# Holding the second group's loads behind most of the output weights, which come in four pieces

## The chip, the core and the metric

The kernel runs on one core of one Trainium2 chip. The metric is the device time of one execution in microseconds; the runs of a kernel are compared by their median. The kernel before was run six times: median 223.87 us, from 222.33 to 224.88 us.

## What is computed

A gated linear attention is followed by a small MLP. There are 4 batches, 8 heads, 768 positions and a head size of 48. Cut to what matters, the reference is:

```python
f = 1.0 / (1.0 + np.exp(-f_logit))
for t in range(S):
    state = f[:, :, t, :, None] * state + np.einsum('bhd,bhe->bhde', k[:, :, t], v[:, :, t])
    y[:, :, t] = np.einsum('bhd,bhde->bhe', q[:, :, t], state)
x = y.transpose(0, 2, 1, 3).reshape(B * S, H * D)      # 3072 x 384
h = x @ w_in                                           # w_in: 384 x 2048
out = (h * sigmoid(h)) @ w_out                         # w_out: 2048 x 384
```

All inputs lie in the chip's memory (HBM) in float32. q, k, v and f_logit have 4.7 MB each, the two weight matrices 3.1 MB each.

## The kernel before, in words

**Groups.** The 768 positions are cut into six groups of 128 (the index g). A group holds all four batches (b from 0 to 3), 512 rows of the MLP. For each group and batch, `logs` and `decays` make the decay factors from f (ACT and TensorE), `scale_k`, `scale_q` and `values` make bf16 copies of k, q and v (POOL, DVE, POOL), `transposes`, `scores`, `outputs` and `state` do the attention, and `turn` lays its result out for the MLP. `mlp_in` multiplies by w_in and applies the SiLU; `mlp_out` multiplies by w_out, copies a row block out of PSUM on ACT and stores it by a DMA that ACT issues.

**Loads of q, k, v and f.** `load` (L84) issues one DMA on SP. In groups 0 and 1 each input comes in two halves, batches 0 and 1 (`FIRST`) and batches 2 and 3 (`SECOND`), 393 KB each; from group 2 on each comes whole, 786 KB. SP issues nothing else, so its order is the order of all these loads: the eight halves of group 0, then by `load_all` (after the `turn` loop) the eight of group 1 in the order f, k, q, v FIRST, f, k, q, v SECOND, then group 2, and so on. One head's row of 48 float32 values is 192 bytes, and that is what a packet of this queue carries. The queue is called q1 in the profile. The tiles `f_ld`, `k_ld`, `q_ld`, `v_ld` have two buffers each, so group 1 can be loaded while group 0 is in use.

**Loads of the weights.** `load_w_in` and `load_w_out` are generators whose DMAs POOL issues; they turn float32 into bf16 on the way. w_in comes in four pieces of 512 columns, w_out in two pieces of eight row blocks each (n from 0 to 7 and from 8 to 15). This queue is q0 in the profile. Its packets carry 1024 bytes (w_in) or 768 bytes (w_out) as written. The first w_in piece is issued after `scale_k(0, 2)`, the rest after `scale_k(0, 3)`.

**Order.** The program is written out in its final order for each engine (`manual_schedule`), and each engine takes its own instructions in that order. Around the change it is: attention of group 0; `mlp_in(0)` for the first two batches, then for the other two; on ACT the table load `exp_ln_tables` and `logs(1, FIRST)`; `mlp_out(0)`, whose row block of one batch needs all sixteen n of w_out in order, two row blocks by itself and then in turns with `prep(1, FIRST)` (`decays`, `scale`, `lasts`), `logs(1, SECOND)`, `attend(1, FIRST)` and the decays of the second half. `interleave_gen` takes from several streams by the share of their cost that is spent.

Of the kernel before, what the change touches and what calls it, by code (L numbers as in the profile page):

```python
# [11 lines left out]
BF16 = mybir.dt.bfloat16  # L12
# [18 lines left out]
def chain(*gens):  # L31
    for gen in gens:
        yield from gen
# [8 lines left out]
def kernel(  # L42
# [10 lines left out]
    nc = tc.nc  # L53
# [7 lines left out]
    NT = d_ff // 128  # L61
    MT = B * C

    singles = ctx.enter_context(tc.tile_pool(name="singles", bufs=1))
# [14 lines left out]
    def load(g, name, b0=0, b1=B):  # L79
        if (g, name) not in loaded:  # L80
            loaded[g, name] = ld.tile([C, B, H, D], F32, name=f"{name}_ld", tag=f"{name}_ld")
        t = loaded[g, name]
        src = SRC[name].rearrange("b h s d -> s (b h) d")[g * C:(g + 1) * C, b0 * H:b1 * H]
        nc.sync.dma_start(out=t[:, b0:b1].rearrange("p b h d -> p (b h) d"), in_=src)  # L84
# [16 lines left out]
    w_out_sb = singles.tile([128, NT, d_model], BF16)  # L101
    triu = singles.tile([C, C], BF16)
    ident = singles.tile([C, C], BF16)
    ones = singles.tile([C, 1], BF16)
    zeros = singles.tile([C, NP * 2 * D], BF16)

    def load_w_in():
        src = moe_w_in.rearrange("(ko ki) n -> ki ko n", ki=128)
        for n in range(0, d_ff, 512):
            nc.gpsimd.dma_start(out=w_in_sb[:, :, n:n + 512], in_=src[:, :, n:n + 512])  # L110
            yield

    def load_w_out():
        src = moe_w_out.rearrange("(ko ki) n -> ki ko n", ki=128)
        for n in range(0, NT, 8):
            nc.gpsimd.dma_start(out=w_out_sb[:, n:n + 8, :], in_=src[:, n:n + 8, :])
            yield

    def exp_ln_tables():
        nc.scalar.preload_act_table_set("natural_log_exp_and_others")  # L120
# [5 lines left out]
    def logs(g, lo, hi):  # L126

        f = loaded[g, "f"][:, lo:hi]
        nc.scalar.activation(f, f, AF.Exp, scale=-1.0)  # L129
        nc.scalar.activation(lf[g % 3][:, lo:hi, :, 0:D], f, AF.Ln, bias=1.0)  # L130

    def decays(g, b):

        cs = cps.tile([C, H, D], F32, name="cs", tag="cs")
        nc.tensor.matmul(cs, triu, lf[g % 3][:, b, :, 0:D], start=True, stop=True)  # L135
        ias[b] = wk.tile([C, H, D], F32, name="ia", bufs=4)
        nc.scalar.activation(ias[b], cs, AF.Exp, scale=1.0)  # L137
        aas[b] = wk.tile([C, H, D], F32, name="a", bufs=4)
        nc.scalar.activation(aas[b], cs, AF.Exp, scale=-1.0)  # L139

    def scale_k(g, b):
        nc.gpsimd.tensor_mul(ki[g % 2][:, b, :, 0:D], loaded[g, "k"][:, b], ias[b])  # L142

    def scale_q(g, b):
        nc.vector.tensor_mul(qg[g % 2][:, b, :, 0:D], loaded[g, "q"][:, b], aas[b])  # L145
# [6 lines left out]
    def values(g, b, engine=None):  # L152
        src, dst = loaded[g, "v"][:, b], vb[g % 2][:, b]
        if engine is nc.scalar:
            nc.scalar.copy(dst, src)
        else:
            nc.gpsimd.tensor_copy(dst, src)  # L157
# [39 lines left out]
    def evac(engine, dst, src):  # L197
        if engine is nc.scalar:
            nc.scalar.copy(dst, src)
        else:  # L200
            nc.vector.tensor_copy(dst, src)  # L201
# [19 lines left out]
    def turn(g, b, engine=None):  # L221

        x_ps = yps.tile([128, KT, C], BF16, name="x_ps", tag="yd")
        for t in range(KT):
            nc.tensor.transpose(x_ps[:, t, :], ysb[b][:, 128 * t:128 * (t + 1)], ident)  # L225
        if g not in xT:
            xT[g] = gk.tile([128, KT, B, C], BF16, name="xT")
        evac(engine, xT[g][:, :, b, :], x_ps)
# [73 lines left out]
    def mlp_cost(lo, hi):  # L302
        return (hi - lo) * 4 * 650.0
# [11 lines left out]
    def prep_cost(lo, hi):  # L315
        return (hi - lo) * 1000.0 + 100.0
# [5 lines left out]
    def warm(n):  # L322

        w_ps = hps.tile([128, MT], F32, name="w_ps", tag="h_ps")
        for _ in range(n):
            nc.tensor.matmul(w_ps[:, 0:NP * 2 * D], zeros[:, 0:128], zeros, start=True, stop=True)
# [19 lines left out]
    def run(*streams):  # L346
        for _ in interleave_gen(*streams):
            pass

    def load_all(g, names="fkqv", *spans):  # L350
        for span in spans or (ALL,):
            for name in names:
                load(g, name, *span)

    with tc.manual_schedule():
        exp_ln_tables()
        nc.vector.memset(zeros, 0.0)
        nc.vector.memset(ones, 1.0)
        make_upper_triangular(nc, triu, 1.0, diag=True)
        make_identity(nc, ident)  # L360
        for t in (lf[0], qg[0], ki[0], lf[1], qg[1], ki[1], lf[2]):
            nc.vector.memset(t[:, :, :, D:64], 0.0)
        for b in range(B):
            nc.gpsimd.memset(st[b], 0.0)
        w_in, w_out = load_w_in(), load_w_out()


        warm(12)
        logs(0, *FIRST)
        for b in range(*FIRST):  # L370
            decays(0, b)
            warm(2)
            scale_k(0, b)
            scale_q(0, b)
        for b in range(*FIRST):
            values(0, b)
        logs(0, *SECOND)
        for b in range(*FIRST):
            transposes(0, b)
            warm(2)  # L380
        for b in range(*FIRST):
            scores(0, b)
            warm(3)
        decays(0, 2)
        scale_k(0, 2)
        next(w_in)
        outputs(0, 0, nc.scalar)
        decays(0, 3)
        scale_k(0, 3)
        outputs(0, 1, nc.scalar)  # L390
        for _ in chain(w_in, w_out):
            pass
        lasts(0, *ALL)
        scale_q(0, 2)
        scale_q(0, 3)
        for b in range(*FIRST):
            turn(0, b, nc.scalar)
        load_all(1, "fkqv", FIRST, SECOND)
        load_all(2)
        transposes(0, 2)  # L400
        warm(2)
        transposes(0, 3)
        for b in range(*SECOND):
            values(0, b, nc.scalar)


        in0 = mlp_in(0, *FIRST)
        scores(0, 2)
        run((part(in0, 650.0), 650.0))
        scores(0, 3)  # L410
        run((part(in0, 650.0), 650.0))
        outputs(0, 2)
        run((part(in0, 650.0), 650.0))
        outputs(0, 3)
        turn(0, 2)
        run((part(in0, 650.0), 650.0))
        turn(0, 3)
        run((in0, 2600.0))
        run((mlp_in(0, *SECOND), mlp_cost(*SECOND)), (states(0, *ALL), B * D_COST))


        exp_ln_tables()
        logs(1, *FIRST)
        out0 = mlp_out(0, *ALL)
        run((part(out0, 4550.0), 4550.0))
        run((part(out0, 2600.0), 2600.0), (prep(1, *FIRST), prep_cost(*FIRST)))
        logs(1, *SECOND)
        run((out0, 3250.0), (attend(1, *FIRST), attend_cost(1, *FIRST)),
            (chain(wait(1500.0), prep(1, *SECOND, False)), 1500.0 + prep_cost(*SECOND)))
        scales(1, *SECOND)  # L430
        load_all(3)
        att = attend(1, *SECOND)
        half = attend_cost(1, *SECOND) / 2
        run((mlp_in(1, *FIRST), mlp_cost(*FIRST)), (chain(wait(600.0), part(att, half)), half + 600.0))
        exp_ln_tables()
        logs(2, *ALL)
        run((mlp_out(1, *FIRST), mlp_cost(*FIRST)), (att, half),
            (chain(wait(1300.0), prep(2, *ALL, False)), 1300.0 + prep_cost(*ALL)))
        scales(2, *ALL)


        for g in range(1, NCH):
            span = SECOND if g == 1 else ALL
            first = [(mlp_in(g, *span), mlp_cost(*span))]
            if g + 1 < NCH:
                att = attend(g + 1, *ALL)
                total = attend_cost(g + 1, *ALL)
                half = total * 0.54
                first.append((part(att, half), half))
            run(*first)  # L450
            second = [(mlp_out(g, *span), mlp_cost(*span))]
            if g + 1 < NCH:
                second.append((att, total - half))
            if g + 2 < NCH:
                exp_ln_tables()
                logs(g + 2, *ALL)
                lead = 4000.0 if g == 1 else 2000.0
                second.append((chain(wait(lead), prep(g + 2, *ALL, g > 1)), lead + prep_cost(*ALL)))
            run(*second)
            if g == 1:  # L460
                scales(g + 2, *ALL)
            if 2 <= g + 3 < NCH:
                load_all(g + 3)
# [30 lines left out]
```

## Time and profile before

| | |
|---|---|
| median of the six runs | 223.87 us |
| the profiled execution's own time | 222.38 us |
| its span, first to last instruction | 220.6 us |
| mean granted TensorE clock in it | 0.969 |
| TensorE busy with matmuls | 188.4 us, 85% of the span |
| ACT, DVE, POOL busy | 126.2, 104.5, 46.4 us |
| moved by DMA | 27.00 MB; q1 18.88, q10 (stores) 4.72, q0 (weights) 3.15 |

The profile is of one execution. "The span in 40 slices" shows the busy share of each engine and of the 16 DMA engines over time. The timeline gives for each run of equal instructions the start, the time from the start of the first to the end of the last, the engine, the line of the kernel, the operation, output and inputs, the count, and in brackets how long the engine had been idle before and what ended that. Of the DMA engines it gives, for a stretch of time, each queue's packets, bytes and the time that its packets took, as a share of sixteen engines over the stretch; packets of one engine overlap, so the shares can sum to more than 100%. The granted clock is the share of full speed at which TensorE was let run.

### The profile page before, as it was taken

How to read it: one execution, taken by the hardware profiler on the slowest of the kernel's cores; microseconds unless marked ns; L12 is line 12 of the kernel's file. 1: busy time of each engine (PE TensorE's matmuls, PEld its weight loads, DVE VectorE, ACT ScalarE, POOL GpSimd, SP SyncE). 2: the span in 40 equal slices, each digit the busy share in tenths (PEclk: the TensorE clock that was granted, in tenths of full speed). 3: DMA queues.
4: the chain of work that ended last, by engine and by line, in shares of the span. 5: the costliest groups of instructions: out<-in, count | busy, mean ns of one | idle time of the engine just before them, and what ended most of it. 6: DMA issues, size and time to landing. Idle time of an engine off the chain costs nothing.

```text
span 220.6 us, 4190 instructions
## 1 busy us (share of the span) xinstructions
PE 188.4 (85%) x1740; PEld 117.1 (53%) x1740; DVE 104.5 (47%) x189; ACT 126.2 (57%) x209; POOL 46.4 (21%) x64
## 2 busy tenths in 40 slices
PE   6486399787778587999799998999998999999993
PEld 2244178554466355865455655555665456643461
DVE  3358352204846438886764666556673446300000
ACT  3438147836174856596667855768647671158421
POOL 4317400006220074007400066000363000000000
PEclk9679769999999999999999999999999999999999
DMA  7999999999999999999999411000011000110011
GB/s 134 187 186 190 194 189 184 197 197 230 214 186 207 176 188 226 183 196 208 210 163 197 63 73 70 5 1 3 36 71 39 0 3 36 39 71 0 0 71 71
DMA packets 105970, 27.00 MB, mean 122 GB/s; under 512 B 99296, under 2 KB 105952, under 8 KB 105952
## 3 DMA queue, kind: packets, MB, share of 16 engines
q1 hardware_dynamic: 98816, 18.88, 58.2%
q0 software_dynamic: 3680, 3.15, 8.7%
q10 hardware_dynamic: 3456, 4.72, 6.3%
q8 instruction: 13, 0.21, 0.4%
q14 instruction: 5, 0.04, 0.1%
HBM read 25.17 MB, written 4.72 MB: 135 GB/s over the span
## 4 chain that ended last, share of the span: by engine, by line
PE 61%; DMA 12%; DVE 11%; ACT 8%; POOL 3%; issue 3%; ACTq 1%; SPq 1%; DVEq 0%
PE o_ps L292 23%; PE h_ps L282 21%; DMA w_out_sb<-in_moe_w_out_dram 9%; DVE qg L145 5%; PE t_ps L178 5%; PE a_ps L188 4%; DMA q_ld<-in_q_dram 3%; DVE qk L180 2%; DVE atm L192 2%; PE y_ps L210 1%; POOL w_in_sb L110 1%; PE y_ps L214 1%; ACT o_sb L297 1%; PE cs L135 1%; PE x_ps L225 1%
## 5 line engine op out<-in xcount | busy, mean ns | idle before, releaser
L282 PE MATMUL h_ps<-xT,w_in_sb 128*128 128x256 bf16 (+1 forms) x384 | 74.8, 332 | 6.2 <-DMA w_in_sb<-in_moe_w_in_dram 3.6
L285 ACT ACTIVATE hT<-h_ps 128x512 bf16<-128x512 f32 x96 | 56.8, 597 | 32.9 <-PE h_ps L282 31.1
L292 PE MATMUL o_ps<-w_out_sb,hT 128*128 128x384 bf16 x384 | 71.9, 326 | 1.7 <-DMA w_out_sb<-in_moe_w_out_dram 1.7
L282 PEld LDWEIGHTS <-w_in_sb 128*128 128x128 bf16 x384 | 35.2, 99 | 28.5 <-issue 6.2
L142 POOL TENSOR_TENSOR ki<-k_ld,ia 128x384 bf16<-128x384 f32 x24 | 24.9, 1038 | 119.3 <-ACT ia L137 93.7
L292 PEld LDWEIGHTS <-hT 128*128 128x128 bf16 x384 | 34.9, 97 | 26.3 <-issue 6.7
L192 DVE TENSOR_TENSOR atm<-a_ps,triu 128x512 bf16<-128x512 f32 x48 | 30.9, 686 | 19.8 <-PE a_ps L188 19.8
L145 DVE TENSOR_TENSOR qg<-q_ld,a 128x384 bf16<-128x384 f32 x24 | 22.8, 977 | 22.4 <-ACT a L139 16.2
L297 ACT COPY o_sb<-o_ps 128x384 f32<-128x384 f32 x24 | 11.5, 478 | 26.7 <-PE o_ps L292 26.7
L180 DVE COPY qk<-t_ps 128x1024 bf16<-128x1024 bf16 x24 | 16.6, 690 | 18.4 <-PE t_ps L178 18.4
L137 ACT ACTIVATE ia<-cs 128x384 f32<-128x384 f32 x24 | 11.8, 491 | 20.9 <-PE cs L135 17.2
L240 DVE TENSOR_TENSOR st<-d_ps,al 48x192 bf16<-48x192 f32 x40 | 14.1, 353 | 15.9 <-PE d_ps L236 15.6
L157 POOL CAST vb<-v_ld 128x384 bf16<-128x384 f32 x22 | 15.3, 697 | 1.2 <-DMA v_ld<-in_v_dram 1.2
L135 PE MATMUL cs<-lf,triu 128*128 128x384 bf16 x24 | 7.9, 331 | 8.1 <-ACT lf L130 4.5
L178 PE MATMUL t_ps<-ident,qg 128*128 128x128 bf16 x96 | 9.7, 226 | 5.4 <-DVE qk L180 3.6
L201 DVE CAST y<-y_ps 128x384 bf16<-128x384 f32 x22 | 12.2, 553 | 4.5 <-PE y_ps L214 4.3
L178 PEld LDWEIGHTS <-qg 128*128 128x128 bf16 x96 | 7.5, 100 | 10.8 <-issue 5.4
L129 ACT ACTIVATE f_ld<-f_ld 128x768 f32<-128x768 f32 (+1 forms) x8 | 9.3, 1162 | 6.9 <-DMA f_ld<-in_f_logit_dram 6.8
L188 PE MATMUL a_ps<-qk 48*128 48x128 bf16 x192 | 10.0, 226 | 2.9 <-DVE atm L192 2.9
L139 ACT ACTIVATE a<-cs 128x384 f32<-128x384 f32 x24 | 11.6, 484 | 0.0
L214 PE MATMUL y_ps<-vb,atm 128*128 128x48 bf16 x192 | 11.6, 186 | 0.0
L188 PEld LDWEIGHTS <-qk 48*128 48x128 bf16 x192 | 5.7, 97 | 11.1 <-issue 7.0
(40 smaller groups left out, 143.3 us busy)
## 6 DMA issues: line engine op xcount, KB each, us to landing
out_dram<-o_sb ACTq DMA_DIRECT2D x24, 192.0 KB, 1.9
f_ld<-in_f_logit_dram SPq DMA_DIRECT2D x4, 768.0 KB, 11.0
k_ld<-in_k_dram SPq DMA_DIRECT2D x4, 768.0 KB, 11.4
q_ld<-in_q_dram SPq DMA_DIRECT2D x4, 768.0 KB, 11.0
v_ld<-in_v_dram SPq DMA_DIRECT2D x4, 768.0 KB, 10.8
f_ld<-in_f_logit_dram SPq DMA_DIRECT2D x4, 384.0 KB, 6.7
k_ld<-in_k_dram SPq DMA_DIRECT2D x4, 384.0 KB, 7.6
q_ld<-in_q_dram SPq DMA_DIRECT2D x4, 384.0 KB, 6.6
```

The lines of the kernel that those rows point to most:

```text
L142: nc.gpsimd.tensor_mul(ki[g % 2][:, b, :, 0:D], loaded[g, "k"][:, b], ias[b])
L145: nc.vector.tensor_mul(qg[g % 2][:, b, :, 0:D], loaded[g, "q"][:, b], aas[b])
L157: nc.gpsimd.tensor_copy(dst, src)
L178: nc.tensor.transpose(t_ps[:, j, p, :], src[i][:, b, 2 * p:2 * p + 2, :], ident)
L180: nc.vector.tensor_copy(sb, t_ps)
L188: nc.tensor.matmul(a_ps[:, r, p, :], qkT[b][lo:lo + D, 1, p, :], qkT[b][lo:lo + D, 0, p, :], start=True, stop=True)
L192: nc.vector.tensor_mul(sb[:, r], a_ps[:, r], triu[:, None, :].to_broadcast([C, NP, C]))
L214: nc.tensor.matmul(y_ps[:, 2 * p + r, :], atm[b][:, r, p, :], vb[i][:, b, 2 * p + r, :], start=not opened, stop=True, skip_group_check=True)
L240: nc.vector.tensor_mul(st[b][lo:lo + D, :, r * D:(r + 1) * D], d_ps[lo:lo + D, :, r * D:(r + 1) * D], alast[g][lo:lo + D, b, :, None].to_b ...
L282: nc.tensor.matmul(h_ps[:, j], w_in_sb[:, kk, (n + j) * 128:(n + j + 1) * 128], xT[g][:, kk, lo:hi].rearrange("p b c -> p (b c)"), start=( ...
L285: nc.scalar.activation(hT[g][:, n:n + per, lo * C:hi * C], h_ps, AF.Silu)
L292: nc.tensor.matmul(o_ps, hT[g][:, n, b * C:(b + 1) * C], w_out_sb[:, n, :], start=(n == 0), stop=(n == NT - 1))
```

## The change

w_out comes in four pieces of four row blocks in place of two of eight. A one-row tile `behind` of 64 bf16 values is added. After group 0's `turn` loop, and ahead of `load_all(1, ...)`, SP issues a DMA of 128 bytes from w_out's row block 10 into that tile. Row block 10 is in the third piece (n from 8 to 11), so this DMA waits until that piece has landed, and with it every later load on SP's queue waits. Nothing reads `behind`.

```diff
@@ -102,6 +102,7 @@
     ones = singles.tile([C, 1], BF16)
+    behind = singles.tile([1, 64], BF16)
     zeros = singles.tile([C, NP * 2 * D], BF16)
@@ -112,8 +113,8 @@
     def load_w_out():
         src = moe_w_out.rearrange("(ko ki) n -> ki ko n", ki=128)
-        for n in range(0, NT, 8):
-            nc.gpsimd.dma_start(out=w_out_sb[:, n:n + 8, :], in_=src[:, n:n + 8, :])
+        for n in range(0, NT, 4):
+            nc.gpsimd.dma_start(out=w_out_sb[:, n:n + 4, :], in_=src[:, n:n + 4, :])
             yield
@@ -395,6 +396,9 @@
         for b in range(*FIRST):
             turn(0, b, nc.scalar)
+
+
+        nc.sync.dma_start(out=behind, in_=w_out_sb[0:1, 10, 0:64])
         load_all(1, "fkqv", FIRST, SECOND)
         load_all(2)
```

## The prediction

> **What bounds the kernel now.** I read the 40 slices first: TensorE is at 9 tenths from about 60 us to the end, the DMA engines from the start to about 121 us. A change in the loads can show only where TensorE waits for one. The waits between 20 and 60 us name two such places: the first w_in piece (3.6 us, ending at 26.19) and the second half of w_out. The timeline of PE shows the second:
>
> ```profile
> 40.73 0.81 PE L282 MATMUL h_ps<-xT,w_in_sb 128*128 128x256 bf16 x6
> 41.40 1.46 PE L292 MATMUL o_ps<-w_out_sb,hT 128*128 128x384 bf16 x8
> 44.52 4.06 PE L292 MATMUL o_ps<-w_out_sb,hT 128*128 128x384 bf16 x24 [1.65 <-DMA w_out_sb<-in_moe_w_out_dram]
> 48.41 0.33 PE L135 MATMUL cs<-lf,triu 128*128 128x384 bf16 x1
> ```
>
> The first eight matmuls use row blocks 0 to 7, then PE stands until the second half has landed. Matmuls of this run follow each other every 0.162 us (24 from 44.52 to 48.41), so eight need 1.3 us, and the start-to-start loss is 44.52 - 41.40 - 1.3 = 1.8 us. ACT in the same stretch:
>
> ```profile
> 42.20 1.28 ACT L120 ACT_TABLE_LOAD   x1
> 43.49 0.84 ACT L129 ACTIVATE f_ld<-f_ld 128x768 f32<-128x768 f32 x1
> 44.37 0.84 ACT L130 ACTIVATE lf<-f_ld 128x768 bf16<-128x768 f32 x1
> 46.01 0.48 ACT L297 COPY o_sb<-o_ps 128x384 f32<-128x384 f32 x1 [0.80 <-PE o_ps L292]
> ...
> 48.61 0.48 ACT L297 COPY o_sb<-o_ps 128x384 f32<-128x384 f32 x1 [2.12 <-PE o_ps L292]
> ...
> 49.56 0.49 ACT L137 ACTIVATE ia<-cs 128x384 f32<-128x384 f32 x1 [0.47 <-PE o_ps L292]
> ```
>
> Here ACT waits for PE, not for loads: f FIRST of group 1 landed at 21.7 (issued 14.90, 6.8 to landing) and is first used at 43.49. That slack of 22 us is what the change spends. POOL says when the weights are issued and when k and v of group 1 are used:
>
> ```profile
> 18.57 0.93 POOL L110 DMA_DIRECT2D w_in_sb<-in_moe_w_in_dram  x1
> ...
> 22.80 1.78 POOL L116 DMA_DIRECT2D w_out_sb<-in_moe_w_out_dram  x2
> 50.14 0.99 POOL L142 TENSOR_TENSOR ki<-k_ld,ia 128x384 bf16<-128x384 f32 x1 [25.55 <-DMA out_dram<-o_sb]
> 51.09 0.82 POOL L157 CAST vb<-v_ld 128x384 bf16<-128x384 f32 x1
> ```
>
> **What the queues cost each other.** The DMA view of three stretches: 12 to 18 us (q1 alone), 26 to 31 (w_in beside q1), 34 to 42 (w_out beside q1).
>
> ```profile
> q1 hardware_dynamic: 5872, 1.12, 144.6%
> ```
> ```profile
> q0 software_dynamic: 806, 0.79, 93.2%
> q1 hardware_dynamic: 810, 0.16, 27.8%
> ```
> ```profile
> q0 software_dynamic: 1535, 1.17, 92.8%
> q1 hardware_dynamic: 1536, 0.29, 33.5%
> ```
>
> Both queues send equal numbers of packets: they take turns, and as q0's are four to five times larger, w_out already has most of the time. Per engine (a sixteenth of the packets): q1 alone one packet every 6 us / 367 = 16.4 ns; a w_in packet with its q1 partner 5 / 50.4 = 99 ns; a w_out packet with its partner 8 / 95.9 = 83 ns.
>
> With q1 held, q0 runs alone, which this trace never shows. **Bounds for a w_out packet alone:** 83 ns if q1 only filled gaps; 83 - 16.4 = 67 if the partner took what it takes alone; 54 if q0's packets overlapped as q1's do alone (92.8% of 8 us over 95.9 packets is 77 ns each, by 1.45). For w_in: 99, 83, 64. I take the middle ones; the nearest row, q1 alone, prices the partner that goes.
>
> **When the third piece lands (T).** w_in is 1536 packets, 96 per engine, w_out 2048, 128 per engine. q0's first packets move at 21.9 (POOL's issue at 18.57 plus 3.3), and it loses 0.9 us near 24.5 between the first two pieces; I keep both. Middle: 96 x 83 ns = 8.0, 128 x 67 = 8.6, plus 0.9: last packet at 39.4, the third piece's 32 x 67 = 2.1 earlier, 37.3. From last packet (about 43.3) to PE's start (44.52) it took 1.2, so **T = 38.5**. Slow end: the halves landed at 39.0 (22.80 + 16.2) and 44.5, so three quarters stand at 41.8. Fast end: 96 x 64 + 128 x 54 = 13.1, plus 0.9, less 1.7, plus 1.2: 35.4.
>
> **The parts.** 1. *Four pieces for two*: two more issues of 0.9 us on POOL, until 26.4. POOL's next work is at 50.14, so nothing; without that cover 1.8 us. Row blocks 8 to 11 no longer wait for 12 to 15.
>
> 2. *w_out earlier*: in the middle case T is 38.5 and the fourth piece lands at 40.6, before PE needs them (42.7 and 43.3). The 1.8 us stall goes. At the slow end the fourth still lands at 44.5 and about 1.2 of it stays.
>
> 3. *w_in earlier*: the first piece saves 24 x 16 ns = 0.4 us, but TensorE's granted clock from 24.5 to 31.4 is 0.5, so starting 0.4 sooner saves 0.2 of full-speed work. Together **2.0**.
>
> 4. *The hold*: behind SP's waiting DMA stand all later loads; stores go by ACT's queue and are free. f FIRST lands at T + 0.4 (issue of the small DMA, from the first f_ld issue) + 4.0 (shortest f_ld issue to landing) = 42.9. With everything 2 us earlier on PE, ACT is free for the logs at about 43.3: no wait. After them come 0.84 + 0.84, the copies and store issues of two row blocks, and `ia`; `ia` follows PE's second row block and has 0.85 us of room. So f costs nothing up to T = 39.75, eats the gain one for one after that, and at T = 41.75 nothing is left. k, q, v FIRST follow at 2.1 us each (393 KB at 187 GB/s): 45.0, 47.1, 49.2, wanted at 48.1, 48.5 and 49.1, so v is even. The second four land at 51.3, 53.4, 55.5, 57.6. f SECOND is wanted at 50.4, but what needs it, `ia` of batch 2, is at 56.6; k at 57.1 and v at 58.1 are in time. Group 2 took 18 us after v SECOND (53.5 to 71.5) and is then complete at 75.6; its v is wanted at 76.6. Later groups have more room. Sum of the hold: 0 in the middle case. At the slow end f FIRST lands at 46.2 and `ia` is at 49.6, as before; v FIRST lands at 52.5, 1.4 after POOL wanted it (51.09), and `ki` of batch 1 waits behind it; from nothing to 1.0 of that reaches PE, as TensorE has the transposes of batch 0 and four MLP matmuls in between.
>
> Sum: -2.0 us; bounds -2.4 (fast end: w_in's first piece 24 x 35 ns = 0.8 sooner, worth 0.4) and +1.0 (slow end). The profiled execution has 222.38, giving 220.4; the median is 1.49 above that execution, and the same 2.0 from it gives **221.9**.
>
> **Two rules of the skill.** The page DMA: Bandwidth & Descriptors, Rules for kernel authors, says to issue a DMA early and wait for it late; by it the hold, which gives up f's 22 us of cover, should cost time. The row of f's landing at 21.7 agrees that the cover is there; by my sum it isn't all needed. Its section Bandwidth fits a POOL-issued DMA as 2.0 us plus bytes at 436 GB/s; by that w_in and three quarters of w_out (2.75 MB) would, as an estimate, take 8.3 us and T would be about 27 to 30, and the hold free by a wide margin. The 34 to 42 row, 1.17 MB in 8 us beside q1, doesn't look like it.
>
> **Rivals.**
> *The hold eats it.* q0 is paced by its own packets (93% of the time with packets of its own speaks for that) and hardly quickens: T between 40.6 and 41.8. The stall goes, and `ia` is late by as much. A milder form: in the median execution PE reaches `mlp_out` 1.5 us later than in the profiled one and the stall is only 0.3. Either gives about -0.4: 223.5.
> *Slower: f is late.* Place: ACT, waiting in `logs(1, FIRST)` with the two PSUM copies behind it, and PE behind `ia`. From T = 41.75 each us costs one. If the small DMA is released only by all of w_out at an unchanged pace, T = 44.5 and the price is 2.75: 226.6; halfway 225.3. For: q1's starts are then all at once late, v FIRST past 52. Against: PE's start at 41.40 shows that waits go by pieces, and q1's 28 to 34% share must come free somewhere.
> *q0 much faster alone* (54 ns): PE gains only 0.4 more, since the stall can't go twice: 221.5. Counted with the forecast.
>
> **Numbers.** Forecast 0.60, hold eats it 0.20, slower 0.20. About 0.5% (1.1 us) is what a measurement of this kernel tells from no change; the forecast lies beyond it, the first rival inside, the second beyond on the other side. Range: down to the fast end less the 0.6 us by which such medians may differ, 220.9; up into the slower rival to 225.4. If the forecast's mechanism holds, 221.3 to 222.6.
>
> **What the changed profile would show.** Right: PE's 32 matmuls from 41.2 in one piece; q0's packets alone from 22 to about 39.5, w_out every 67 ns per engine; no wait of ACT at `f_ld` near 43.3; `cs` of group 1 near 46.5. Wrong: SP's f_ld issue after 42; an ACT idle entry "DMA f_ld"; POOL waiting for v_ld near 50 or 77. A clock step at another time would move all of this alike and prove nothing.

## The result, and the profile after

The changed kernel has a median of 220.66 us (28 runs, 218.60 to 223.34); the kernel before, beside it and over all its runs, 224.19 us (63 runs). The ratio is 0.988, 95% interval 0.986 to 0.991: about 2.6 us faster (2.0 to 3.2), where 2.0 was forecast. The ratio compares the executions of each kernel that lie within 1.5% of its quickest, which is why it says less than the 3.5 us between the two medians. The profiled execution took 220.56 us with a span of 218.8, 1.8 less than before.

PE's timeline of the changed kernel, to be laid beside the four lines of before:

```profile
24.23 0.83 PE L283 MATMUL h_ps<-xT,w_in_sb 128*128 128x256 bf16 x6 [1.88 <-DMA w_in_sb<-in_moe_w_in_dram]
...
27.96 1.46 PE L283 MATMUL h_ps<-xT,w_in_sb 128*128 128x256 bf16 x6 [1.22 <-DMA w_in_sb<-in_moe_w_in_dram]
...
41.00 5.36 PE L293 MATMUL o_ps<-w_out_sb,hT 128*128 128x384 bf16 x32
46.20 0.33 PE L136 MATMUL cs<-lf,triu 128*128 128x384 bf16 x1
```

The wait for w_out is gone: 32 matmuls in one piece, and `cs` of group 1 at 46.20 instead of 48.41. `mlp_out` itself begins only 0.4 us earlier. The last 64 matmuls of the kernel, before and after:

```profile
206.71 10.56 PE L292 MATMUL o_ps<-w_out_sb,hT 128*128 128x384 bf16 x64
```
```profile
204.48 10.56 PE L293 MATMUL o_ps<-w_out_sb,hT 128*128 128x384 bf16 x64
```

So the 2.2 us gained at `cs` reach the last matmuls unchanged. The span is only 1.8 us shorter, as it ended 3.2 us after the last store was issued and not 2.8.

SP's timeline shows the hold, and ACT's what it costs:

```profile
37.57 0.58 SPq L401 DMA_DIRECT2D behind<-w_out_sb  x1
38.19 0.57 SPq L84 DMA_DIRECT2D f_ld<-in_f_logit_dram  x1
```
```profile
43.09 0.84 ACT L130 ACTIVATE f_ld<-f_ld 128x768 f32<-128x768 f32 x1
...
47.35 0.49 ACT L138 ACTIVATE ia<-cs 128x384 f32<-128x384 f32 x1 [0.48 <-PE o_ps L293]
...
51.00 0.84 ACT L130 ACTIVATE f_ld<-f_ld 128x768 f32<-128x768 f32 x1 [0.71 <-DMA f_ld<-in_f_logit_dram]
```

Group 1's loads are released at 37.57 and the first f is used at 43.09 without a wait. f of the SECOND half is 0.7 us late, and POOL waits 1.4 us for v SECOND (its `vb` at 59.31). Neither reaches PE: the next `ia` on ACT is at 56.37, 2.2 us sooner than before.

The DMA view from 30 to 36 us has one queue left, which is w_out almost alone:

```profile
q0 software_dynamic: 1601, 1.21, 130.7%
```

1601 packets in 6 us are 100 per engine, one every 60 ns, against 83 with a partner.

### The profile page after: what moved, and what is told of

Read it like the earlier page. It is cut to its first block, busy times and chain, and to the rows that moved or that the text cites. A ratio compares the mean times of both kernels' runs of the same rounds, so it can differ in the third digit from the quotient of the medians.

```text
span 218.8 us, 4193 instructions
## 1 busy us (share of the span) xinstructions
PE 189.1 (86%) x1740; PEld 117.6 (54%) x1740; DVE 104.5 (48%) x189; ACT 126.1 (58%) x209; POOL 47.6 (22%) x66
## 4 chain that ended last, share of the span: by engine, by line
PE 68%; DVE 11%; ACT 8%; DMA 6%; issue 3%; POOL 1%; ACTq 1%; SPq 1%; DVEq 0%
PE h_ps L283 27%; PE o_ps L293 24%; DVE qg L146 5%; PE t_ps L179 5%; PE a_ps L189 4%; DMA w_in_sb<-in_moe_w_in_dram 3%; DMA q_ld<-in_q_dram 3%; DVE qk L181 2%; DVE atm L193 2%; PE y_ps L215 2%; PE x_ps L226 2%; PE y_ps L211 1%; ACT o_sb L298 1%; PE cs L136 1%; ACT a L140 1%
## 5 line engine op out<-in xcount | busy, mean ns | idle before, releaser
L283 PEld LDWEIGHTS <-w_in_sb 128*128 128x128 bf16 x384 | 35.4, 100 | 28.1 <-issue 6.0
L241 DVE TENSOR_TENSOR st<-d_ps,al 48x192 bf16<-48x192 f32 x40 | 14.1, 353 | 16.4 <-PE d_ps L237 16.1
L202 DVE COPY xT<-x_ps 128x384 bf16<-128x384 bf16 x22 | 7.7, 356 | 8.2 <-PE x_ps L226 7.8
```

Of the source, the lines that this page charges most:

```text
L283: nc.tensor.matmul(h_ps[:, j], w_in_sb[:, kk, (n + j) * 128:(n + j + 1) * 128], xT[g][:, kk, lo:hi].rearrange("p b c -> p (b c)"), start=( ...
```

## The experiments

Two theories were set against the forecast's own. The **queue theory** is the forecast's: group 1's packets slowed the weights, the hold removes them, and PE's wait for w_out goes. The **piece theory** says that the finer pieces alone do it. The **w_in theory** says that the gain is w_in's earlier landing (its first piece starts PE at 24.23 instead of 26.19), not w_out's. Ratios are to the kernel before on the same chip. "cs" is the start of the first `cs` matmul of group 1, the first point behind `mlp_out`'s two row blocks.

| kernel | mlp_out starts | PE waits for w_out | cs | ratio (95% interval) |
|---|---|---|---|---|
| before | 41.40 | 1.7 | 48.41 | |
| before_again | 40.58 | 2.2 | 48.13 | |
| the change | 41.00 | 0 | 46.20 | 0.988 (0.986 to 0.991) |
| after_again | 39.26 | 0 | 44.46 | 0.989 (0.985 to 0.994) |
| e1 pieces only | 40.48 | 1.7 | 47.52 | 0.995 (0.990 to 0.999) |
| e2 hold only | 40.53 | 0 | 47.61 | 0.997 (0.992 to 1.002) |
| e3 hold to w_in | 40.90 | 0 | 46.09 | 0.985 (0.979 to 0.991) |
| e4 f twice | 39.53 | 0 | 44.73 | 0.985 (0.979 to 0.991) |
| e8 f ahead once | 39.24 | 0 | 44.43 | 0.985 (0.980 to 0.990) |
| e6 longer hold | 38.44 | 0 | 47.02 | 1.016 (1.012 to 1.020) |
| e10 early w_in, no hold | 38.85 | 1.1 | 45.31 | 0.985 (0.979 to 0.991) |
| e7 early w_in | 37.56 | 0 | 42.76 | 0.979 (0.973 to 0.985) |
| e9 early w_in, hold to w_in | 37.74 | 0 | 42.93 | 0.977 (0.971 to 0.983) |
| e11 early w_in, f ahead | 37.84 | 0 | 43.03 | 0.988 (0.981 to 0.994) |

In the recorded executions of e2 and e3 POOL's first weight issue was 1.3 us later than in the changed kernel's (19.7 instead of 18.4); PE's matmuls ran at about half pace in both up to 30.6 us (four `t_ps` in 0.63 us, in the changed kernel 0.39), although the view gives a granted clock of 1.00 there. In e6's it was 0.5 us sooner (17.9). The table has the times as recorded; where the text takes the 1.3 us off, it says so.

**The pieces alone (e1).**

```diff
-        nc.sync.dma_start(out=behind, in_=w_out_sb[0:1, 10, 0:64])
```

> w_out in four pieces, no hold. Queue theory (the hold gives w_out the DMA engines; that removes PE's 1.8 us stall): q1 goes on beside w_out, the third piece lands near 41.8 and the fourth near 44.5, PE still waits some 1.2 us of the 1.8, w_in is as before. Gain 0.6 us, ratio 0.997, PE wait on w_out 1.0 to 1.4 us. Piece theory (the finer pieces alone let PE run on): PE wait under 0.3 us, gain 1.6 to 2.2, ratio 0.990 to 0.993. w_in theory (the gain is w_in's earlier first piece): no gain, 0.999 to 1.001, and PE's w_in wait stays 3.6 us.

PE's timeline of e1:

```profile
40.48 2.11 PE L293 MATMUL o_ps<-w_out_sb,hT 128*128 128x384 bf16 x12
44.28 3.41 PE L293 MATMUL o_ps<-w_out_sb,hT 128*128 128x384 bf16 x20 [1.69 <-DMA w_out_sb<-in_moe_w_out_dram]
```

Now twelve row blocks run before the wait instead of eight, and the wait is as long, because PE came 0.9 us sooner than in the profile of before and the last piece landed when the second half does in before and before_again, near 44.3. The piece theory falls. The four row blocks that no longer wait are still worth something: `cs` is 0.6 us sooner than in before_again and 0.9 sooner than in before, where the queue theory gave the pieces 0.6; the ratio leaves room for a gain of 0.1 to 1.0%.

**The hold alone (e2).**

```diff
-        for n in range(0, NT, 4):
-            nc.gpsimd.dma_start(out=w_out_sb[:, n:n + 4, :], in_=src[:, n:n + 4, :])
+        for n in range(0, NT, 8):
+            nc.gpsimd.dma_start(out=w_out_sb[:, n:n + 8, :], in_=src[:, n:n + 8, :])
```

> The hold with w_out in two pieces, so that SP waits for the second half. Queue theory: the second half lands near 39.5, before PE needs it (42.5), f of group 1 FIRST lands near 44.5, up to 1.4 us after ACT is free, of which 0.85 is hidden: gain 1.6 to 2.2 us in the profile, ratio 0.988 to 0.992. Piece theory: no gain or a loss of up to 0.3%, 1.000 to 1.003. w_in theory: the same ratio as the changed kernel, 0.988. Also: if q0's weak stretch from 22.5 to 25.6 us in the changed kernel comes from POOL still issuing w_out, it ends near 24.4 here.

The stall is gone, and most of the gain with it. ACT's timeline of e2:

```profile
41.32 1.28 ACT L121 ACT_TABLE_LOAD   x1
45.85 0.84 ACT L130 ACTIVATE f_ld<-f_ld 128x768 f32<-128x768 f32 x1 [3.24 <-DMA f_ld<-in_f_logit_dram]
...
49.32 0.49 ACT L138 ACTIVATE ia<-cs 128x384 f32<-128x384 f32 x1 [0.47 <-ACT o_sb L298]
```

With 1.3 us taken off, the release is at 39.7 and f lands at 44.6, as expected. But ACT was free at 42.6, 41.3 by the same count, since PE had reached `mlp_out` at 39.2 by it; so f was 3.2 us late and not 1.4. `ia` at 49.32 is 48.0 by the same count: 2.2 us behind after_again's 45.86, where PE reaches `mlp_out` at 39.26 too, and only 1.3 ahead of before_again's 49.28. I had missed how little room is left when PE is quick. From POOL's first weight issue to the release it took 21.3 us, against 19.2 in the changed kernel: half w_out is one quarter more to wait for (32 packets per engine x 60 ns = 1.9 us). So the pieces do matter, but for the hold: they let it end a quarter sooner. Where q0's weak stretch near 24 us comes from this run didn't settle.

**A hold that ends with w_in (e3).**

```diff
-        nc.sync.dma_start(out=behind, in_=w_out_sb[0:1, 10, 0:64])
+        nc.sync.dma_start(out=behind, in_=w_in_sb[0:1, 0, 1536:1600])
```

> Four pieces, but SP's small DMA reads the last columns of w_in, so the hold ends when w_in is in, near 32 us, and group 1's loads share the engines with w_out. Queue theory: w_out alone to about 33.5 at 60 ns a packet per engine, then 83 ns with a partner: last piece near 41.5, before PE needs it near 43; no PE wait on w_out and the whole gain, ratio 0.987 to 0.990, with f landing near 36. If the hold must cover w_out: PE waits 0.5 us or more on w_out and a quarter or more of the gain is lost, 0.991 to 0.995. w_in theory: same as the changed kernel, 0.988, even where a PE wait on w_out is seen.

SP's timeline of e3, then PE's:

```profile
33.16 0.59 SPq L401 DMA_DIRECT2D behind<-w_in_sb  x1
```
```profile
40.90 5.36 PE L293 MATMUL o_ps<-w_out_sb,hT 128*128 128x384 bf16 x32
```

SP releases at 33.16, w_out shares the engines from then on, and still PE has no wait for it; e9 below shows the same. So the hold need not cover most of w_out. In these runs it was enough to give w_in and the start of w_out the engines.

**f ahead of the hold (e4, e8).** In e4 a `load(1, "f", *FIRST)` stands ahead of the small DMA, but the list behind it issues the same load again, and ACT waited for that one (until 42.93). e8 issues it once.

> As the change, but f of group 1 FIRST is issued ahead of the hold, right behind group 0, and moves from about 19 to 21 us. Queue theory: w_in's first packet comes up to 1.5 us later, w_out's third piece near 39 and no stall; mlp_in starts near 25.5, which costs 0.2 to 0.5; ratio 0.989 to 0.991. w_in theory: w_in's first wait goes back towards 3.6 us and half or more of the gain goes, ratio 0.994 or above. If ACT's wait for f were a hidden cost of the change, this kernel would be faster than it by 0.3% or more, 0.985 or below.

> f of group 1 FIRST issued ahead of the hold and only once (in e4 the held list issued it a second time, and ACT waited for that one). It lands near 21.5 and ACT has no wait for it. Queue theory: no stall on w_out, w_in's first packet late by up to 1 us; the same as the changed kernel within the measurement, 0.985 to 0.991. If a wait for f still costs the changed kernel time in most executions: 0.983 or below. w_in theory: 0.992 or above.

```diff
+        load(1, "f", *FIRST)
         nc.sync.dma_start(out=behind, in_=w_out_sb[0:1, 10, 0:64])
-        load_all(1, "fkqv", FIRST, SECOND)
+        load_all(1, "kqv", FIRST)
+        load_all(1, "fkqv", SECOND)
```

Both are where the change is. ACT's timeline of e8 has no wait for f FIRST:

```profile
41.32 0.84 ACT L130 ACTIVATE f_ld<-f_ld 128x768 f32<-128x768 f32 x1
```

The time is the same within the intervals (0.985 and 0.988), so the change loses nothing by f's landing that these runs can measure. Against the w_in theory these two say nothing, as the extra load held w_in up by little: PE began it at 24.40 and 24.57.

**A longer hold (e6).** Two more small DMAs, each reading what the last one wrote, stand ahead of group 1's loads.

```diff
-        nc.sync.dma_start(out=behind, in_=w_out_sb[0:1, 10, 0:64])
+        nc.sync.dma_start(out=behind[0], in_=w_out_sb[0:1, 10, 0:64])
+        for i in range(2):
+            nc.sync.dma_start(out=behind[i + 1], in_=behind[i])
```

> The change with a longer hold: two more small DMAs, each reading what the one before wrote, stand between the release and group 1's loads; one took 3.2 us from issue to landing, so the loads start 6 to 6.5 us later than in the changed kernel, f of group 1 FIRST lands near 49. Queue theory with the slack that the prediction worked out: ACT waits some 6 us for f, the first ia of group 1 is at 52.5 to 53 instead of 47.4, and of the 6.4 us at most 1.1 is hidden: ratio to the kernel before 1.010 to 1.016. If other work covers late loads (the hold was never near the path): 0.988 to 0.997.

The two links added 3.7 us, not 6.4 (36.69 to f's issue at 40.99, instead of 0.6 us). ACT's timeline, PE's, and the stretch from 46 to 56 us (busy time of each engine, granted clock, DMA) of e6:

```profile
45.26 0.84 ACT L130 ACTIVATE f_ld<-f_ld 128x768 f32<-128x768 f32 x1 [4.74 <-DMA f_ld<-in_f_logit_dram]
```
```profile
47.02 0.32 PE L136 MATMUL cs<-lf,triu 128*128 128x384 bf16 x1 [3.22 <-ACT lf L131]
```
```profile
46.00:56.00 10.00, 7.11 (x41) 3.82 (x41) 2.33 (x3) 5.26 (x11) 3.11 (x4) 0.66 1.34 212
```

PE stands 3.2 us at `cs`, and then its clock is granted at 0.66 over the next 10 us (the same stretch of the changed kernel: 1.00, of after_again: 0.86). PE had reached `mlp_out` 0.8 us sooner than in after_again, and is 3.7 us behind it at ACT's table load for group 2's logs (73.80 and 70.14): 3.7 us of hold cost about 4.5. "Never near the path" falls, and 1.6% is the size that the queue theory gave, but for a hold of 6.4 us. The recorded execution (225.32 us) is the quickest of the ten; what the slower ones (to 229.54) lose besides isn't shown.

**w_in sooner (e7, e9, e10, e11).** PE's remaining wait in the changed kernel is for w_in. POOL is idle from about 12 us until `scale_k(0, 2)` at 17.4:

```diff
         decays(0, 2)
+        next(w_in)
         scale_k(0, 2)
         next(w_in)
         outputs(0, 0, nc.scalar)
```

The first piece is then issued at 12.1 instead of 18.4 us, and the second 1.8 us sooner (18.5 instead of 20.3). e7 is this with the change, e9 this with e3's hold, e10 this without a hold, e11 this with e8's loads.

> The change, with w_in's first piece issued on POOL ahead of scale_k(0, 2) and the second ahead of scale_k(0, 3). Queue theory: PE's remaining wait for w_in (3.1 us in two parts) falls to under 1.5, mlp_in starts near 23 and PE reaches mlp_out 0.5 to 1.5 us sooner, while the hold's release moves by less; then f is late by up to 1 us, of which 0.85 is hidden. Ratio 0.981 to 0.987. Rival: the early pieces take packets from group 0's last loads, ki and vb of batch 2 and 3 come later by as much, and nothing is gained: 0.987 to 0.992.

> As e7, with the hold ending at w_in's last piece as in e3. Queue theory: f of group 1 lands 3 to 5 us sooner than in e7 and is never late, w_out still lands in time (e3 showed no wait on it), so all of e7's sooner start reaches the end: ratio 0.979 to 0.985, at or under e7. If w_out alone on the engines is needed once PE is sooner: a PE wait on w_out of 0.5 us or more, and 0.985 to 0.990.

> e7 without the hold: w_in's first two pieces early, w_out in four pieces, group 1's loads where they were before. Queue theory: q1's packets go on beside w_out, the fourth piece lands near 43, PE reaches mlp_out near 38 to 39 and then waits 2 to 4 us for w_out, so most of the early start is handed back there: ratio 0.990 to 0.997. w_in theory (the sooner start of mlp_in is what counts): 0.978 to 0.983, as e7.

> e7 with f of group 1 FIRST once and ahead of the hold, as e8. Queue theory: ACT has no wait for it (0.7 us in e7's profile), f SECOND comes 2 us sooner; w_in and w_out give up at most 1 us to the 393 KB. Within the measurement of e7 and e9: 0.974 to 0.983. If the extra load ahead of w_in delays PE: a PE wait on w_in of 1 us or more, 0.983 to 0.987.

PE's timeline of e7, then of e10:

```profile
23.68 1.46 PE L283 MATMUL h_ps<-xT,w_in_sb 128*128 128x256 bf16 x6
...
37.56 5.36 PE L293 MATMUL o_ps<-w_out_sb,hT 128*128 128x384 bf16 x32
42.76 0.33 PE L136 MATMUL cs<-lf,triu 128*128 128x384 bf16 x1
```
```profile
42.06 3.41 PE L293 MATMUL o_ps<-w_out_sb,hT 128*128 128x384 bf16 x20 [1.10 <-DMA w_out_sb<-in_moe_w_out_dram]
45.31 0.33 PE L136 MATMUL cs<-lf,triu 128*128 128x384 bf16 x1
```

In e7 no wait for a weight is left, and `cs` is 3.4 us ahead of the changed kernel's and 1.7 ahead of after_again's. e7 and e9 beat both kernels, with ratios of 0.979 and 0.977. Without the hold (e10) the wait for w_out is back, with waits for w_in of 1.2 us, and `cs` is 2.6 us later than in e7; in the whole time the intervals of e10 and e7 overlap. e10 did better than I expected, as w_out landed at 42.0 rather than 43. So the w_in theory is right in part: weights that are issued sooner gain time without any hold, and e10's 0.985 is no worse than the change's 0.988, though here w_out comes sooner with them. e11 starts as e7 does (`cs` 43.03), but its recorded execution had two further stretches at half clock (52.0 to 55.4 and 72.5 to 75.9) and ended 2.5 us after e7's; its interval overlaps both e7's and the change's, so whether f ahead costs anything there stays open.

**The same two kernels once more.**

> The changed kernel once more, beside the others. Queue theory: no PE wait on w_out, first w_in packet about 1.9 us after POOL's issue, PE at w_in near 24.3, f of group 1 in time or up to 1 us late; half-clock stretch of TensorE after that wait of 3.4 or 6.8 us, whichever way its windows fall. Ratio 0.985 to 0.991. If the gain came from the particular clock windows of the recorded execution: 0.993 or above.

> The kernel before once more, for a second look at its start. Queue theory: w_out's second half lands 25.9 us after POOL's first weight issue (44.5 and 18.57 in the first look), whenever PE comes to it, so cs of group 1 is at 47.5 to 48.5 again; if TensorE's half-clock stretch after the w_in wait is 3.4 us instead of 6.8, PE reaches mlp_out near 40.5 and its wait for w_out grows to 2.3 to 2.9 us. If the stall was an accident of the first look: no wait on w_out, or under 0.5 us, and cs before 47.

before_again and after_again, PE's timeline, and the stretch from 24 to 32 us with its granted clock:

```profile
44.23 4.06 PE L292 MATMUL o_ps<-w_out_sb,hT 128*128 128x384 bf16 x24 [2.19 <-DMA w_out_sb<-in_moe_w_out_dram]
48.13 0.33 PE L135 MATMUL cs<-lf,triu 128*128 128x384 bf16 x1
```
```profile
24.00:32.00 8.00, 6.72 (x66) 4.98 (x66) 3.05 (x7) 2.85 (x5) 0.49 (x1) 0.79 1.22 196
```
```profile
39.26 5.36 PE L293 MATMUL o_ps<-w_out_sb,hT 128*128 128x384 bf16 x32
44.46 0.33 PE L136 MATMUL cs<-lf,triu 128*128 128x384 bf16 x1
```
```profile
24.00:32.00 8.00, 7.14 (x69) 5.54 (x70) 3.03 (x7) 3.37 (x6) 1.66 (x3) 0.79 1.18 180
```

In this pair the half-clock stretch was 3.4 us long; in the first pair 6.8 (the same row shows 0.57 before and 0.61 after). Before, that makes no difference to `cs`: 48.41 and 48.13, since PE waits for w_out there whenever it comes. After, it does: 46.20 and 44.46 (PE's wait for the second w_in piece, 1.2 us in the first pair, is also missing in the second). The gain at `cs` is 2.2 us in the one pair and 3.7 in the other, on both sides of the 2.6 measured over all runs. In the first pair 1.8 us of it are the stall and 0.4 the sooner start of `mlp_out`, in the second 2.4 and 1.3. No run holds the loads back for w_out alone, so how the measured gain divides between w_out and w_in is known from these two pairs only.

In after_again f FIRST was late, as ACT's timeline shows:

```profile
42.38 0.84 ACT L130 ACTIVATE f_ld<-f_ld 128x768 f32<-128x768 f32 x1 [1.04 <-DMA f_ld<-in_f_logit_dram]
```

Most of that is hidden: PE's second `cs` comes 2.32 us after the first, against 2.07 in the changed kernel's other recording.

## Why the prediction was right, and where its sizes were off

*The stall (part 2).* Right. It was forecast to go and went, at 41.00 in one run of 32 matmuls (forecast 41.2). e1 shows that it takes the hold, e3 that it doesn't take all of it.

*The queues' prices and T.* The release came at 37.6, forecast 38.5, bounds 35.4 to 41.8. A w_out packet alone takes 60 ns, forecast 67: the partner cost more (23 ns) than it takes alone (16.4). A w_in packet alone took 81 ns between 26 and 29 us (593 packets), forecast 83. That T came within 0.9 us is in part luck: q0's packets began 1.7 us sooner than I had kept (20.2 us) and three quarters of w_out took 0.7 us less (96 x 7 ns), but the first half of w_in's packets took 0.9 us more (to 26.1), and the release came 1.7 us after three quarters of w_out's packets had moved (35.9), not 1.2. The fast end of the sum has a slip: its 0.4 us for w_in takes the place of the 0.2 and isn't added to it, so the bound should have been -2.2, not -2.4.

*w_in earlier (part 3).* This is the mis-sized term, and the likeliest reason for a gain of 2.6 us and not 2.0, which lies at the edge of the interval. I kept q0's first packet at 21.9 us, 3.3 us after POOL's issue, and let w_in gain 0.4 us at half clock. In fact the first piece went from issue to landing in 5.8 us instead of 7.6, as the two rows of DMA issues show, before and after:

```profile
w_in_sb<-in_moe_w_in_dram POOLq DMA_DIRECT2D x1, 384.0 KB, 7.6
```
```profile
w_in_sb<-in_moe_w_in_dram POOLq DMA_DIRECT2D x1, 384.0 KB, 5.8
```

In the second pair it is 6.8 and 6.2. q0's first packet moved 1.6 us after POOL's issue in both recordings of the changed kernel, and 3.0 and 2.6 us after it in those of the kernel before. So part of the 3.3 us was a queue of q1's packets ahead of q0's first ones, and PE began w_in at 24.23, not 25.8. In the recorded execution little came of that, because the second piece was waited for (1.2 us) and the clock stayed at half for 6.8 us. I also took that stretch as fixed; it was 3.4 us in after_again and in e4, e6 and e8. With the hold, what PE gains there passes on to `cs`; without it w_out's landing takes it back, as before_again shows. That the 2.6 us lies between the two pairs because executions of both kinds are in the median is argued, not shown; the clock's share was not tried alone.

*The hold (part 4).* Right in its working: f at 42.7 (forecast 42.9), no wait on ACT, v and f SECOND late by about a microsecond and hidden. ACT waiting for f and POOL for v were to be signs of being wrong, and after_again has both, 1.0 us for f FIRST and 1.1 us for v near 48.5; the room of 0.85 us took most of f's wait and 0.25 reached PE, about as the sum's working has it. e8 shows no cost of f that can be measured, e2 that the room is small: one quarter of w_out later, the gain was 0.3% with zero inside its interval, which is the picture of the first rival.

*The slower rival.* Its place was right (e6: ACT in the logs, PE behind it). Its break-even point, a release at 41.75, was too generous for the whole kernel: e6's f was issued at 40.99, a release of 40.6 by the prediction's count, and `ia` at 48.74 is still 0.8 ahead of before (41.3 and 0.1, if the 0.7 us by which e6's weights were issued sooner than before's come off). So up to `ia` the sum holds; yet the whole is 1.6% slower. The prediction had compared single times of before and priced the wait alone. It left out that PE, which reached `mlp_out` sooner in every other recorded execution than in the profiled one of before, then has more to wait, and that the clock goes down after the wait. How much each of the two has of the 1.6% stays open.

*The milder form of the first rival*, that the stall is small in most executions, finds no support: it was 1.7, 1.7 and 2.2 us in before, e1 and before_again, and before_again (224.98 us) is slower than the median.

*The two rules of the skill.* The page DMA: Bandwidth & Descriptors says, in Rules for kernel authors, to issue early. Here the early loads were 22 us early and took 23 ns from every w_out packet, which was needed sooner; e6 shows the rule's side, where the hold outgrows the cover. Its fit for POOL's DMAs stands in the section Anatomy of one DMA — SWDGE (gpsimd) path, not in Bandwidth. By it T would have been, as an estimate, 27 to 30; it was 37.6. The fit counts one number of bytes; these loads read two bytes for each one they write, and w_in and three quarters of w_out read 5.5 MB, which by the fit is an estimate of 14.6 us from the first issue, against 19.2 measured.

## What to carry to other kernels

A prefetch that uses the same DMA engines as a load that is needed sooner isn't free, even when it gets few of the bytes: look at the DMA queues of the stretch in which the compute engine waits, and hold the prefetch back by a small DMA that depends on the urgent load, for just as long as that load needs. Work out how much later the held data may land, and end the hold well before that point, since in e6 a late load cost its wait and then some clock. Then look at the wait that is left: here one weight piece issued in POOL's idle time, and the next 1.8 us sooner, took the ratio from 0.988 to 0.979; without any hold the same issues gave 0.985, as much as the hold alone gave.

## What the runs showed of the hardware that I had not expected

- Two queues on the same engines moved equal numbers of packets, 1535 and 1536 in 8 us, so bytes went by packet size: 1.17 MB to 0.29.
- A backlog on one queue delayed the first packets of another: the first w_in piece took 5.8 and 6.2 us from issue to landing without (the change and after_again), 7.6 and 6.8 (before and before_again) with it.
- TensorE's half-clock stretches were 3.4 or 6.8 us long in different executions of one kernel, around waits of 1.7 to 3.6 us for w_in; e7 had one of 3.4 us at 22 us although PE's waits in the 4 us before it were all under 0.8 us, and further ones of 3.4 us appeared in some executions between 51 and 91 us. That they are a good part of why runs of one kernel differ by some 2 us is likely, but not shown.
- A small DMA that waits for the one before it was issued 2.2 and then 1.6 us after that one (e6).
